# Thirty-three loads issued by ScalarE instead of SyncE, in a gated linear attention kernel with a low-rank mixer and an MLP behind it

## The chip, the cores and the metric

The kernel runs on one core of a Trainium2 chip. The metric is device time in microseconds (us) of one execution, the median of several runs. The engines that compute are TensorE (PE), VectorE (DVE), ScalarE (ACT) and GpSimd (POOL); SyncE (SP) computes nothing and issues transfers. Each engine works through its own stream of instructions in order; semaphores tie the streams together. An instruction that starts a transfer (a DMA) stands in the stream of the engine that issues it, and the transfer itself is carried out by 16 DMA engines.

## What is computed

The batch is 4, with 8 heads, 768 steps and a head size of 48, so that the model's width is 384. A recurrence with a gate per channel is followed by a mixing over time with a matrix of rank 32 and an MLP of width 1536:

```python
for t in range(S):
    state = alpha[:, :, t, :, None] * state + np.einsum('bhd,bhe->bhde', k[:, :, t], v[:, :, t])
    y[:, :, t] = np.einsum('bhd,bhde->bhe', q[:, :, t], state)
x = y.transpose(0, 2, 1, 3).reshape(B, S, H * D)
h = x.transpose(0, 2, 1) @ U @ V
u = x + h.transpose(0, 2, 1)
out = u + np.maximum(u @ w_ch1, 0.0) @ w_ch2
```

Inputs and output are float32; the matmuls run in bfloat16.

## The kernel before

**Tiles.** The sequence of each batch is cut into six chunks of 128 steps. Every chunk needs four tiles of 128 x 384 float32 (192 KB each): alpha, k, q and v. The four batches have 96 such tiles. 24 more tiles of the same size bring the MLP's weights (12 for `w1`, 12 for `w2`), and U and V come in four small transfers. All tiles of this size, and the output's, live in a pool `io` of 40 slots; a load that takes a used slot waits until the last reader of the tile that lay there is done.

**A chunk's work.** Two forms of the recurrence exist. `stage_pair` handles the first chunks of batches 0 and 1 (six and four chunks: the list `PAIRS`); its tiles are loaded with rows of two steps (L332, "paired" in what follows). `stage_gla` handles the others (L339, "unpaired"). In both, ScalarE takes the logarithm of alpha (Ln, L362 or L534), TensorE sums it up over the chunk, ScalarE takes Exp of the sum with both signs (L385 and L386, or L551 and L552), and VectorE or GpSimd multiplies k and q by these (L393 or L562). The products `rkq` are transposed to `kqt`: by TensorE and an eviction (L411, L576, then a copy), except for batch 3, whose six transposes are done by the DMA engines (L588). Then come the scores (L435, L604), their masking on VectorE (L446, L614), the update of the state (L469, L627, and what follows), and the output y (L508, L518, L666, L671), which is evicted to `xb`.

**Behind the recurrence.** `stage_mix` mixes over time with U and V (L686, L716, and for batch 0 L705 and L708) and brings `uT`, the transpose that the MLP reads; for batch 3 this transpose is done by the DMA engines (L722). `mlp1` has 24 groups of three matmuls of 128 x 384 for each batch (L767), each evicted with Relu by ScalarE (L777) or VectorE (L779). `mlp2` has for each chunk twelve matmuls in three groups (L793), a sum on VectorE (L799) and the store of the output (L802, L804): two stores of 96 KB for a paired chunk, one of 192 KB for an unpaired one, and the very last chunk is split in two column ranges.

**What sets the order.** The functions do not emit instructions: each adds steps to a list (`Plan.add`, with the engines that could do the step). A step is a function with its engine to be chosen; it may emit one instruction or a group of matmuls. A text `TABLE`, written in advance, then lists all 1071 steps, three characters each: two name the step and one its engine. A second text `SLOTS` gives the slot of each buffer at its first use. `Plan.run` walks through the table and emits. Thus the table sets the order of every engine's stream; between engines only the semaphores count, so that an engine may be far ahead of another one's place in the table. SyncE, which waits for nothing but free slots and finished results, can be far ahead with its loads. In the kernel before, all 123 loads, the nine transposes and the 35 stores are in SyncE's stream, 167 entries.

Lines to follow: `weight` (issue on L305, its conversion to bfloat16 by L273 on ScalarE or L277 on GpSimd), `stage_loads` (L332 and L339), `copy` (L273 on ScalarE, L275 on VectorE, L277 on GpSimd).

Of the kernel before, what the change touches and what calls it, by code (L numbers as in the profile page):

```python
# [15 lines left out]
TABLE = """
A8SCcABASCzABQSETACePChACfAA+SCgACjDC1PC4AC3AC2AEVPEYABISA9SCiDCkPCmDClPBBSC5GEXADjADlPDnAEWACnDDmACoPCqDA-SCdGCrPCsDBDS
C0GDCPBCSC6GC7PBESCvPCpDC8PC+DDKACtPCuDCwPCxDDDDC9AC-PDADDBDABSAFGAGPAHDAJPAKADMPDPABKSCyDDEPDNADGPDFDDqGDsPBJSDpGDrPDtA
DuDDHPDJADZPBYSG2ABSSEaGBHSDLGDoAEcPDyPEeADIDBFSDQGDaPDbDDSPDUDDvPDwDBMSBLSDkGDzPD0DDxDG4PD8AD+PBRSEZGEbPEdDD3PDcPDdDDOA
BGSDRGDTPDVDG5AEAAD1PD2DBUSGfABOSEDGEfPEhDEgDD-AG7ABNSECGEBAG6ABTSBcSEUABPSD9GGhPGiAGjAGkAD4PELPBVSBWSGlGGmGBgSBXSGgGAAS  # L20
ADGBZSG8GAiSAjGAQSAeSAfGAgSAhGDWPDXDEiPD5PD7ABkSD6AEjPEkDEFPEEPEHAHNADYDEGDElPEMPENDAOSAPGARGEmPDfPAMSANGDePEnPEoADgPDiD
DhAAYSAZGBaSG9GAWSAUSAVGEIPEJDEKDHmAHPPHSAEPPGnPAXGASSATGHQABdSHTGBbSG3GEpAHRABiSBfSHOGAaSBhSBeSBoSAcSAkSBlSBjSAmSBpSAoS
BqSBmSGoPGqDGpDEOPAqSBnSHoPHrAEQPESDAuSAsSGuPGvDGwDEqPGrPGtDGsDERAErPHpAHqAHtGE8PE5PAwSAySEwPG+PHADE2PBrSEsAExPEyAE6PE7D
FFPE9PE+DA2SE3PEtPEzPFBPFCDFHPEuPFJPFGDE4AEvAE0PE1AF1PH-AFIDGyPF5PF3PF4DE-PFADFfPFgDF6AF2AFDPFhPFiAGxDFlPFmAFdPA4SACSFED
A0SFKDFLPFMAFNPFODG-PFjPFkAFeDA6SFVPFWAIBPICAFRPFSAHUGHBDHCPHDDAdGBsSGzPIEAIDAHFPFtPHGDHHDHIGIGGG0AAbAFuAHVPHXAG1AFnPHJP
B0SBwSBySB4SB8SFPPBuSBzSFQAHEDHKPHLAHMAHcPHdDHeDHsDIFAIVAFTPFUAFoAFrPFsAFpPHvPFqDHfDHxAHWPIXPIYAHuPHwDFvPFwDFZPFaDFzPF0D
HYAHiPHZPHbDHaDIZAAnAHyPHzDIHDFbPApAFcAHhPFxPFyAFXPHjPHkAHlAFYAHnGH1PH2DH3DH4DIIPIKAH6PAlGIaGIcPIbGIdPIfAIJPArGGTPIeAH7P
GNPH0DH8PH+AILDIMPH9DIODIgPIhDGBPIAGIPPH5GIRDF7PGZPHgGAzGAtAAvAAxAGOPINDITPF8PIQDIiDISGIWAIjPA5GGaPA3AGCPIUAAEGIkAIlPImD
GUPA1GA7AGbPGcDIvPIwDALGIzPI0DI1PI2DF9PF+DItPIuDGDPKLAGPPInPIpPIqDGEDKNPK0AI3PIxPIyDIoDKfAKOAI4AKPAKhPKjAKnGGVPGWDK2PK3A
LJAKlAJfPJgALeAKRAIrPIsDJRPJjPJSAJkDJdPJeAKiAKkAK6AKQAI5PJHPJIDJPPJQAJLPJMAI-PJAAK5AK4ALgPLkAJFPJGDJJPJKDLjABxSKmGKoPKqA  # L30
JTPJUDI6DKTGKVPJnPJoDLiALhABvSKMGBtSKSGKgAKUPJXPKWDKXDKbPKcDJlPLLPLMAJYDJbPJmAB9SB2SK8GKvPJBPK+PKwDKxDLAACASJcDJDPJEAB1S
KpPKrDGQDLOAK7GLNAJCAI9PI+ALPACESK9PK-DCMSNlAI7PI8DJVPJWALzAB3SK1GKsPKuDLBPLDDLCDKYPKZDJvPJNPJOAB6SLRGLTPLVAJhPL1PL2AL3A
B+SCCSB5SLHPLIANnPNqAB-SKtDLfALlGLnPKaDJwPL5GLQDCBSL4GLEPNrAKyPKzAJiAOIAB7SLKALpAGHPJZPGIPLSPLUAJaALFDLGGLmGKBPL6PL8DGJP
L7PGKDL9ALoPLqACNSCISCFSNoANsGLZPLaDJxPJyDNpACGSNtGKCPCKSCLSCQSCUSCDSLWPLXDL+PLrPKdPKeALYDLtDKDPJ7PLuPN2AN4PN5AJ8PJpPLbG
LsDLvDL-DLwGMADL0GOaAOcPOgAOfAOdACHSNmGN3GLcPN6ALdAN+GJ9PLxPLyDKEDMBPJqPNuSNvPNwDMCAMDPJrPOeAGMSNxDJ+DMEAN7AN8AOKPOMAAIG
MTPMUDMNPJ1PMLPMRPKGPMODJsDMMDCSSCRSOhGNyPNzDN0PMHPMIDKHPMFPMGDOsAOuPKIPMPPMQAMSDMJPMKDOOAMVPMWDKJDJ2PCWSOvAOLAMfPMXPMYD
J3PMjPM7POiGCYSO+AGFSCTSGGSPAPN1AONAObGGYSCJSCXSOtGCaSGSSKFSGLSN9GOwACPSOjSCVSOzGO0DOPDMkDMgDOxAOyAPBAPCAMbPMcDMpPMqAMlP
MmAJ4DNBPODPNDPMZPM-POEDMaAM8ANCACOSOQGNADM1PM2AOkPM5PNEDMxPMyAN-SM9PMhPM3PM4AJuSF-SMtPM6AMuAOJGOVPCZSPDGPEDOmDOlDOFDOWD
OXGMdPMeDM+AOnPOoDOpGNFPNGDMnPMoAMvPMiAOqPOrAOAPOBDO1SO2PO3DO4DOCDORSJ-SOSPOUDNHPMrPMsANRPMzPO5PO6DO7GOTDO8PO9ANSPGRSCbS
O-APFSJ5SPGPM0DPIDPHDGXSOGPOHANTPNUDOYPMwANIPPJPPKAOZAGASNJPNbPPLPNMPNcPPMAPPPPQDPSPPXPPNPPODPRSPYDPTDNdPNKDPUPPVDPWSNWP  # L40
NgPJtSNNPPZPNhPPaDPbSNXPNiPNOPNeDJ6SNPDNQSJzSNVSKASGeSGdSNYPNfSNLSNjDNkSPmPPePPuPPvAPgPPiPPjDPcPP2PPyPPnAQCPNZDNaSPoPPwP
PhAPzAPxAP3DQAPQBAPdAP8PPkPPlDP6PQGPQHAQIPQJDQEPQKPQFAQDAPsPP4PP5AP0PPtDP+PPfAPqPP1DPpAP-AQWPQMPQRPPrDQLDQNPP7AP9AQlPQXP
QSPQqPQYPQZDJ0SKKSQaSQrPQbPQTPQUDQVSQmPQOPQPDQQSQsPQtDQuSQcPQnPQoDQpSQgPQdPQhPQeDQfSQiPQjDQkS
"""
SLOTS = """
AABBCCAAADAABBBBCCEFDAEGBCAFACAGHAHAABAIBDEJCKHABBGABCABBGDDLBCCGMACBHNCODPCAEADQAGCCABFCRSDEDHACTBABUDAAVBWBFBABBXDCYZE
aAGCBACDbcCdeBfAghijEHBBkBFGBCCDlEAmBnABCFHCAGCDCDBFDEDAGHEIJKLMNOPQRSTUBCAVWFDYXHEBAGBCACBBADabHEDFZAAGcCBEAHDFBAECAGBH
EFCdeGBEFfHDAGBCBgFACEHGABCBBAEFijlkhHmnGCBADCAHGCABFDBAEHGBCACBEFADHGACCDBCBECGAHBDCAEDBFBHCCEAGBFHBBBGCBABBGCCHABGBCBF
HBCCAGBDDEAABFBCDHBAHBCFBAHGCCABAFHAGBEBBBEDHEAHBGACFCBIGAAEGACCKHLCJDAAMGOBBHCPCCDAGEBAFCBHQCDDEGACNSRHCABTABDDUCGAVBCF
HGBDCEADWGXYbBAHAaAZcdefgEFBDHGBAAEACFCBBBCACBGCAiEDACDDjHBADBHBkADCAGCAHFDElhFCGCABFCGBCFADmEBAFBADEHBGBABnLAPCQDMBABCB  # L50
ACGIDBFCAAKHGBCECADFHCESDADBBBGAAFCEHABCAGCBBFDAHAGCABBBTEDDABBRFCABEBDAGCFAUBDFCOVNGHBBCAEFBGbADCFBDCEBCEBGEBHGAEBZDYeg
iFd
"""


# [91 lines left out]
def kernel(  # L147
# [37 lines left out]
    nc.scalar.preload_act_table_set("natural_log_exp_and_others")

# [115 lines left out]

    def weight(dst, src, key, engs):
        t = Buf(io)
        P.add({"SP": 545.0}, lambda e: nc.sync.dma_start(flat(t), src), w=[t])  # L305
# [20 lines left out]
    def stage_loads(b):  # L326
        def load(t, src, c):
            if paired(b, c):
                hs, sl = slice((c % 2) * HP, (c % 2 + 1) * HP), slice((c // 2) * 2 * C, (c // 2 + 1) * 2 * C)
                P.add(  # L330
                    {"SP": 775.0},
                    lambda e: nc.sync.dma_start(  # L332
                        t().rearrange("p (h j) d -> p h (j d)", j=2), src[b, hs, sl, :].rearrange("h (p j) d -> p h (j d)", j=2)
                    ),
                    w=[t],
                )
# [2 lines left out]
            P.add({"SP": 1100.0}, lambda e: nc.sync.dma_start(t(), src[b, :, sl, :].rearrange("h t d -> t h d")), w=[t])  # L339
# [518 lines left out]
```

## Time and profile before

| | |
|---|---|
| runs shown | 159.73, 161.85, 162.47 us; median 161.85 |
| span of the profiled execution | 161.6 us |
| instructions in the profile | 4518, of them 1728 matmuls |
| HBM read and written | 23.89 MB and 4.72 MB, 177 GB/s over the span |
| chain of waits, share of the span by engine | PE 54%, SyncE's queue 20%, DMA 14% |

In the profile's lines, PE, DVE, ACT, POOL and SP are the engines, PEld is the loading of weights into TensorE, a "q" behind an engine's name is its issuing side, L332 is line 332, `out<-in` names the tile that is written and the tile or tensor that is read, and "xN" counts instructions. Times are us unless marked ns. A busy share of the DMA engines can come out a little over 1, since their packets overlap. A busy TensorE is not a TensorE at its peak, as the ends of overlapping matmuls are modelled.

### The profile page before, as it was taken

The numbers are of one execution on the slowest core, as the hardware profiler recorded it, in microseconds if no ns is written. First come the engines' busy times: TensorE is split into PE (matmuls) and PEld (weight loads), VectorE is DVE, ScalarE is ACT, GpSimd is POOL, SyncE is SP. The second block draws the span as 40 slices with busy tenths as digits, with TensorE's granted clock in tenths as the row PEclk, the third lists the DMA queues.
The fourth block names the chain that finished last, engine by engine and source line by source line (L and its number), as shares of the span: only waits on it lengthen the run. The fifth ranks groups of instructions, "written<-read, shape, count | busy, mean of one in ns | idle before, by whom it ended". The sixth has DMA issues, their size and how long they took to land.

```text
span 161.6 us, 4518 instructions
## 1 busy us (share of the span) xinstructions
PE 149.2 (92%) x1728; PEld 98.7 (61%) x1728; DVE 105.7 (65%) x232; ACT 90.8 (56%) x234; POOL 66.0 (41%) x104
## 2 busy tenths in 40 slices
...
DMA  4999995999999969889999899999992047840034
GB/s 125 289 312 315 248 250 150 268 336 253 285 229 279 293 130 209 176 176 203 207 195 215 160 189 198 195 226 204 146 204 67 0 81 172 262 146 0 0 129 163
DMA packets 96964, 31.05 MB, mean 192 GB/s; under 512 B 90640, under 2 KB 96912, under 8 KB 96944
## 3 DMA queue, kind: packets, MB, share of 16 engines
q1 hardware_dynamic: 96944, 30.78, 81.2%
...
HBM read 23.89 MB, written 4.72 MB: 177 GB/s over the span
## 4 chain that ended last, share of the span: by engine, by line
PE 54%; SPq 20%; DMA 14%; issue 4%; POOL 3%; DVE 2%; ACT 1%; POOLq 0%; DVEq 0%
PE ps L793 24%; PE ps L767 19%; SPq L332 13%; DMA io<-in_q_dram 5%; SPq L339 3%; DMA kqt<-rkq 3%; DMA io<-in_moe_w_ch_dram 2%; DMA io<-in_k_dram 2%; DMA io<-in_v_dram 2%; PE ps L576 2%; SPq L802 2%; SPq L305 2%; PE ps L604 1%; PE ps L716 1%; DVE pm L614 1%
## 5 line engine op out<-in xcount | busy, mean ns | idle before, releaser
L767 PE MATMUL ps<-uT,w_sb 128*128 128x384 bf16 x288 | 53.2, 326 | 0.4 <-POOL w_sb L277 0.4
L793 PE MATMUL ps<-w_sb,h1t 128*128 128x384 bf16 (+2 forms) x300 | 53.1, 319 | 0.0
L777 ACT ACTIVATE h1t<-ps 128x384 bf16<-128x384 f32 x61 | 27.6, 497 | 23.2 <-PE ps L767 23.1
L793 PEld LDWEIGHTS <-h1t 128*128 128x128 bf16 x300 | 27.1, 97 | 15.6 <-issue 0.8
L767 PEld LDWEIGHTS <-w_sb 128*128 128x128 bf16 x288 | 26.5, 98 | 16.4 <-POOL w_sb L277 1.2
L779 DVE TENSOR_SCALAR h1t<-ps 128x384 bf16<-128x384 f32 x35 | 18.6, 553 | 14.2 <-PE ps L767 14.2
L799 DVE TENSOR_TENSOR io<-ub,ps 128x384 f32<-128x384 bf16 (+2 forms) x25 | 13.3, 533 | 10.2 <-PE ps L793 10.0
L614 DVE TENSOR_TENSOR pm<-ps,maskc 128x512 bf16<-128x512 f32 x28 | 17.7, 682 | 1.1 <-PE ps L604 1.1
L562 POOL TENSOR_TENSOR rkq<-io,ai 128x384 bf16<-128x384 f32 x12 | 11.4, 949 | 13.8 <-DMA io<-in_k_dram 8.5
L717 DVE TENSOR_TENSOR ub<-xb,ps 128x384 bf16<-128x384 bf16 x24 | 12.4, 548 | 4.5 <-PE ps L716 4.3
L446 DVE TENSOR_TENSOR pm<-ps,maskp 128x512 bf16<-128x512 f32 x20 | 13.1, 683 | 2.4 <-PE ps L435 2.4
L562 POOL TENSOR_TENSOR rkq<-io,aa 128x384 bf16<-128x384 f32 x11 | 10.0, 912 | 9.8 <-ACT aa L552 8.4
L273 ACT CAST xb<-ps 128x192 bf16<-128x192 f32 (+1 forms) x27 | 10.3, 404 | 6.3 <-PE ps L671 4.9
L277 POOL CAST rv<-io 128x384 bf16<-128x384 f32 x18 | 9.4, 529 | 10.3 <-DMA io<-in_v_dram 9.3
L277 POOL CAST w_sb<-io 128x384 bf16<-128x384 f32 x16 | 8.0, 518 | 7.5 <-DMA io<-in_moe_w_ch_dram 7.5
L273 ACT COPY kqt<-ps 128x512 bf16<-128x512 bf16 x17 | 9.8, 610 | 1.9 <-PE ps L576 1.2
L275 DVE COPY kqt<-ps 128x512 bf16<-128x512 bf16 x19 | 7.8, 420 | 4.0 <-PE ps L576 2.2
L551 ACT ACTIVATE ai<-ps 128x384 bf16<-128x384 f32 x14 | 6.9, 498 | 5.5 <-PE ps L543 3.6
L411 PE MATMUL ps<-ident,rkq 128*128 128x128 bf16 x80 | 8.2, 237 | 1.6 <-DVE rkq L393 1.0
L393 POOL TENSOR_TENSOR rkq<-io,ai 128x384 bf16<-128x384 f32 x8 | 7.3, 910 | 5.8 <-DMA io<-in_k_dram 5.8
L638 POOL TENSOR_TENSOR st<-sm,tot 128x384 bf16<-128x384 f32 x7 | 5.8, 829 | 6.6 <-DVE sm L654 6.6
L393 POOL TENSOR_TENSOR rkq<-io,aa 128x384 bf16<-128x384 f32 x9 | 8.2, 910 | 0.6 <-DMA io<-in_q_dram 0.3
...
## 6 DMA issues: line engine op xcount, KB each, us to landing
...
```

Source lines behind the costliest of these rows:

```text
L273: nc.scalar.copy(dst, src)
L277: nc.gpsimd.tensor_copy(dst, src)
L332: lambda e: nc.sync.dma_start(t().rearrange("p (h j) d -> p h (j d)", j=2), src[b, hs, sl, :].rearrange("h (p j) d -> p h (j d)", j=2)),
L393: eng.tensor_tensor(jh(dst()[:, :, 0:D]), raw(a), jh(x()), op=ALU.mult)
L446: nc.vector.tensor_tensor(dst, s2, maskp.to_broadcast([C, 2, 2, C]), op=ALU.mult)
L562: eng.tensor_tensor(dst()[:, :, 0:D], a(), x(), op=ALU.mult)
L614: nc.vector.tensor_tensor(pm()[:, :, par, :], s2, maskc.to_broadcast([C, HP, C]), op=ALU.mult)
L767: nc.tensor.matmul(hb()[:, 0:TW], lhsT=w1_sb[:, ct, jt * 128 : (jt + 1) * 128], rhs=u_half(uT, ct, tt, b in QUEUE_U), start=(ct == 0), sto ...
L777: nc.scalar.activation(dst, hb()[:, 0:TW], AF.Relu)
L779: nc.vector.tensor_scalar_max(dst, hb()[:, 0:TW], 0.0)
L793: nc.tensor.matmul(hb()[:, 0 : hi - lo], lhsT=h1()[:, jt, c * C : (c + 1) * C], rhs=w2_sb[:, jt, lo:hi], start=(jt == 0), stop=(jt == NJ - 1),
L799: P.add({"DVE": 468}, lambda e, hb=hb, lo=lo, hi=hi: nc.vector.tensor_tensor(flat(ou)[:, lo:hi], ub()[:, c, lo:hi], hb()[:, 0 : hi - lo], ...
```

## The change

A new helper gives the queue that belongs to a step's engine, and the three load steps may now name ScalarE. The list `SUM_U` takes the place of a test for batch 0 and holds just batch 0, so that nothing changes by it. Everything else is in the two texts, which are replaced as a whole. No step is added or removed, and no tile changes its shape or its way of being loaded.

```diff
+    SUM_U = (0,)
...
+    def queue(eng):
+        return nc.scalar if eng == "ACT" else nc.sync
...
     def weight(dst, src, key, engs):
         t = Buf(io)
-        P.add({"SP": 545.0}, lambda e: nc.sync.dma_start(flat(t), src), w=[t])
+        P.add({"SP": 545.0, "ACT": 450.0}, lambda e: queue(e).dma_start(flat(t), src), w=[t])
...
                 P.add(
-                    {"SP": 775.0},
-                    lambda e: nc.sync.dma_start(
+                    {"SP": 775.0, "ACT": 450.0},
+                    lambda e: queue(e).dma_start(
...
-            P.add({"SP": 1100.0}, lambda e: nc.sync.dma_start(t(), src[b, :, sl, :].rearrange("h t d -> t h d")), w=[t])
+            P.add({"SP": 1100.0, "ACT": 450.0}, lambda e: queue(e).dma_start(t(), src[b, :, sl, :].rearrange("h t d -> t h d")), w=[t])
...
-        if b == 0:
+        if b in SUM_U:
```

Read step by step, the new table differs from the old one in this:

- **Queues.** 33 of the 123 loads are issued by ScalarE: nine tiles of batch 0 (alpha of chunks 0 and 2; q of chunks 0, 2, 3 and 5; v of chunks 3, 4 and 5), two of batch 1 (k and v of chunk 2), ten of batch 2, nine of batch 3, and three tiles of `w2`. Thirteen of them stand in the table ahead of the first MLP group on TensorE. ScalarE's first two entries that concern data are the loads of alpha and q of chunk 0, and the load of chunk 2's alpha follows; they stand behind the table load of its functions (L185), which is emitted first of all.
- **Engines.** Of the steps that compute, ScalarE has 217 (233 before), VectorE 228 (209), GpSimd 86 (89), TensorE 373 as before. Of the 96 evictions of `mlp1`, ScalarE has 54 (61 before) and VectorE 42 (35).
- **Order.** The first MLP group of batch 0 is entry 274 of the table (297 before) and needs 37 of the transfers in the order in which they are listed (38 before). Batch 3's last tile stands on SyncE behind five stores and four DMA transposes (eleven stores, one of them of 192 KB, and five transposes before). Behind the first use of that tile stand 249 matmuls of full width (128 x 384, the split last chunk counted as such) on TensorE, behind that of the old order's last tile 214.
- **Slots.** The slots of all buffers are chosen anew. For each load on ScalarE that takes a used slot, the step that frees it stands at least 73 entries ahead.

More of the change, by code (lines that the diff above doesn't have):

```diff
@@ L16 @@
 TABLE = """
[L17 to L40, printed above, removed]
@@ L41 @@
-NgPJtSNNPPZPNhPPaDPbSNXPNiPNOPNeDJ6SNPDNQSJzSNVSKASGeSGdSNYPNfSNLSNjDNkSPmPPePPuPPvAPgPPiPPjDPcPP2PPyPPnAQCPNZDNaSPoPPwP
-PhAPzAPxAP3DQAPQBAPdAP8PPkPPlDP6PQGPQHAQIPQJDQEPQKPQFAQDAPsPP4PP5AP0PPtDP+PPfAPqPP1DPpAP-AQWPQMPQRPPrDQLDQNPP7AP9AQlPQXP
-QSPQqPQYPQZDJ0SKKSQaSQrPQbPQTPQUDQVSQmPQOPQPDQQSQsPQtDQuSQcPQnPQoDQpSQgPQdPQhPQeDQfSQiPQjDQkS
+BASA8ABISBCSBBSA9SA+ABEACzAC1PC2ACcACePBDSBJSBQSDjADlPC3AC6GC8PCfACiGBKADoAC5DC7PA-SC+DC9DC-PBGABFSBRSBMSCgACjGClPCkPBHS
+BLADnABUSBSADADDBDDKADMPDmABNSC0ADCPBYSCmDCnDDpGC4ADDDCoPDEPCpDCqDDrPDtDBOSBPADPAETAEVPChADOABTABgSDqGDGPDsPDNABWSDuDABS
@@ new lines @@
+BVSBcSAASDHPEWABXSCdGCrPEXADJACsDDFDDvPDwDEYAD8AAQSCtPCvPCwPCyDCxABkSAOSAMSBaSDRGDTPDIACuDDVAAgSDQGAiSD+PD-ADyPAeSEZGDSP
+EBADxDDUDEbPEdDDLGDZPDaPDbDDWPDXDEAADkGDzPD0DDcPDdDBZSGfAGhPGiAGjAEaGEcPEeDD3PDYDD1PBhSD4PD5PEfPEhDASSAYSBiSAUSD2DEgDG2A
+GkAD7AD6AECGEEPEGADfPG4PG6AG7AAWSAcSEDGEFPG5AELPDePHmAElPEiPD9GEMPEHDENDDgPEUGEjPEkDEIPBbSDiABwSEJDEKDBeSEmPEPPHoPEOPAaS
+BjSBdABoSDhDGmGGoPHqAEnPHNAEQPERDGlGGnPESAGpDHPPAFGAJPGqDAGPAHDHpAADGEqPEpAGrPEoAErPGtDHrAGgAGuPGvDGwDEzPGsDAKAE5PEtPEsA
+E6PE0PE1DE8PARGGyPE2PE9PEuPE3PE4DBfABlSE7AFDPBpSEvDEwPBsAE+AGzPG0ABqSBmSAkAAhAExPEyAFEDG1AANGFHPFIDAPGFjPGxDFnPFlPFmDFoD
@@ new lines @@
+FJPFKDFkAHRAFLPH-AAmSAjGAfGFfPFBPFCDAqSAoSAsSFdPG8GG+PFeAHQAAwABnSFgAFMDHADHtDHsGAySAuSF5PBrSFhPF3PF4DF1PHuPHwDFiAA0SACS
+AVAG9GG-PF2AHSAHBAHvPHxDF6DFNPFOAA2SA4SIBPIEAIDAICAKfAHyPHzDATGHCPHEDE-PFADHDDA6AB0SH0DAXGAZAAdGFtPFRPFTPFuAIFAFVPFWAFSA
+CASHUGHWPHYDAbGFzPF0DKhPKjAKiAG3GHFPHGDHHDHnGH1PIVAHIDH2DH3DH4DFpPFqAHTGFxPFyDHVPKkAHXAKlAFvPFUDFwAIXPIZAIYAFrPHJPFsDFXP
+FYAHKPHMAHOGHcPHdDHLDHeDHZPHaDKLAIGGHbDH5GIIPIKAFbPFcAKNPKRAKOAIaGFZPKQAH7PHfDIcPIbGIdPIfDHhPFPPFaDKPAHiPIeAH6PFQAIHGIJP
+ILDArAHjPHlDHkAH8PH9AIgPIhDH+DIMPIODINDAlGAnGFFPFGDBuAApGGTPGNPAtGF7PGBPGZPB8AIAGIPPAxAAzAAvGGUPIWAHgDITPIUAIRDIQDISGGCP
@@ new lines @@
+GaPIiDIjPALGGOPAEGIkAIlPF8PBvSBxSImAItPI1PI2DIvPIwDA7GA5GA3GA1AF9PIpPIqDIuDBzAKgGGPPGQDCESGDPGEDLzAK0AK2PIzPInPIoDBtALeA
+K6AK5AK4AI0DGVPGWDIxPIyAIrPIsDI3PGbPKTGB2SB1ABySCQAB3SJNPLgPLhAI5PI6AI4DGcDF+DLjANlAJHPKmDKSDJTPJnPJoDK3AK7GCCAKoPKqDKMG
+B4SJOAJLPL1PLiAL2AJUDJdPJMDJeDJPPJQDJJPJbPCBSJcDLkAB9AJKAB+SJZPK8DCMAJjPJkACFSI7PI8AL3AJaAOaAJBPJCDB5SCXSCGSKbPKcDK9PK-D
+JhPJDPJXPKvPKwDJiAKnGKpPJIAI-PJADJYDJEALJAB6AKrDK+PLAAKVPJRPJSAKUPKWAJFPJGALLPLPALMAKXDB7SLBPLCDLDDKsPKYPCDALOAKtDLlGKxG
+LNAB-SGHPJlPKZDNnPNqALmGNrALnPGIPLpAJmAKaDI9PNoAI+ANpACUSJVPJWAKuDLoPLqDL5DL4GK1GLEPL6PJ1PCHSKdPKeALFDOcPNsDLrPLtDLsDKyP
@@ new lines @@
+GJPGKDCOACVAKzALQGLKGLRGLZPLSPLUACaSLHPLIDL7PJ2PL9DLGGLaDNtGAIGNuSCISLfAL8ALTPLVAJfPJgDJ3PLuPLbGLvDLwGOsAJ4DOuPOwAOxACNA
+OIACPSCJSLWPLYDLXDOyAL+PMADCKSNmGKBPL0GOdALxPLyAJvPKCPOeACYAOvAN2ALcPLdACLSL-DNyPNzDMBPCWSKDPMCDOfAOKPOgAKEDOLAOPGNvPNxD
+OMAMDPN4PMEAN5ACZANwDOQGORSJ7POJAMHPMIDMNPMTPN6AN3AONAMRPMSDMODJwPN0PMLPJ8PMFPMUDMVPJ9PMMDMPPMGDN1DOtGMJPN+GN9DCbSN-SOzG
+JxPMQDJ+DMWAM-PM3PM4AMKDO0DM1PJyDO1SOOANAAO+AMxPMyDMrPM2DN8AN7AODPNBPOEDMpPGYSCSAOiGMnPMoAMqDCRANCAMjPMkDJpPMZPMaAMsDOSP
+OAPOBDOUDOTDOCDOFDO2PO4DJqPPAPPCAPBAGGSGdSGFSNDPNEAJrPJsDMdPMhPOYPM9PM7PM8AMtPMXPMYAO3DM+AMiAOZDMuDOVPOWDM5POXDM6DMbPMlP
@@ new lines @@
+MmAMvPMfPMcDMgDMzPGSSCTSObAOhGOnPMeAOoDOGPPDGOjSOkPOlDM0AMwAPEGPFSPGPPHDO5POpGO6DNFPKGPO8PO9AKHPNGAOmDOqPOrAO-GNWPO7GPID
+PJPKFSGRSGeSNXPPKAOHDPLPNRPPMAPSPPTDPUPPVDPWSPZPPaDNgPPXPPYDJ-SNMPNbPKIPKJDPbSPPPPQDNNPNSPPNPPODNhPNOPNcPNYPNTPNUDNdPNeD
+QEPNZDQCPQGPQHDNPDNHPQIPQJAJuSPRSPgPPcPPePPfDQFDPdDQDDP8PNiPNjDPsPP+PP-DPmPPiPP4PKASPhDQAPQBANVSKKSGASP9APqPPjDQWPPwPJtS
+GMSGXSNkSPkPNIPPlAP5DF-SP0PP1AJzSPoPPpANJPPnAPrAGLSNfSJ6SPuPPvDP6PQMPP2PP3APxDNKDP7AQNPQXPNLSJ0SPyPNaSQlPQRPPzDNQSQqPQSP
+PtDQYPQTPQUDQKPQrPQZDQaSQOPQPDQVSQLAQsPQtDJ5SQQSQuSQmPQbPQnPQoDQcPQgPQdPQeDQpSQfSQhPQiPQjDQkS
@@ L44 @@
 """
 SLOTS = """
[L46 to L49, printed above, removed]
```

12 lines of the change are left out of this document (8 added, 4 removed).

## The prediction

> **What bounds the kernel now.** I read the page first (spans, busy shares, the DMA digits), then the chain of waits in order of time, then the busy times by stretch, and last the rows of the issuing lines on the DMA queue.
>
> ```profile
> span 161.6 us, 4518 instructions
> ...
> PE 149.2 (92%) x1728; PEld 98.7 (61%) x1728; DVE 105.7 (65%) x232; ACT 90.8 (56%) x234; POOL 66.0 (41%) x104
> ...
> DMA  4999995999999969889999899999992047840034
> ...
> q1 hardware_dynamic: 96944, 30.78, 81.2%
> ```
>
> TensorE is busy for 92% of the span and no other engine comes near. The DMA digits are the second thing to see: nearly all nines for three quarters of the span, then a fall. All of it runs on one queue, q1, which SyncE issues. So there are two candidates for the bound, and the chain tells where each one rules. Its columns are start, length and what the chain ran through.
>
> ```profile
> 1.23 0.49 SPq L332
> ...
> 24.70 1.88 SPq L305
> ...
> 27.58 3.94 DMA io<-in_moe_w_ch_dram
> ...
> 114.06 4.30 DMA kqt<-rkq
> 118.41 0.40 PE ps L604 x8
> ...
> 126.53 0.43 PE ps L686 x6
> ...
> 135.20 11.70 PE ps L767 x72
> ...
> 158.73 0.30 DVE io L799
> ```
>
> Up to 31.5 (27.58 + 3.94) the chain is SyncE issuing loads and the first MLP weight landing: the fill. From then on it is mostly TensorE. Shortly before 118.41 it leaves TensorE again, for batch 3's loads and transposes. After 118.41 it is TensorE to the end, at full density: 72 matmuls in 11.70 us are 0.1625 us each. The last eviction starts at 158.73, so 2.9 us at the end are eviction and store.
>
> ```profile
> core 0: us, PE busy (x) PEld busy (x) DVE busy (x) ACT busy (x) POOL busy (x), PEclk, DMA share, GB/s
> 0.00:31.60 31.60, 24.22 (x461) 18.41 (x461) 23.46 (x72) 21.21 (x58) 19.80 (x39) 1.00 0.92 242
> 31.60:105.00 73.40, 72.66 (x850) 48.09 (x849) 53.93 (x108) 52.28 (x137) 38.43 (x57) 1.00 0.98 220
> 105.00:118.40 13.40, 12.11 (x107) 7.15 (x105) 9.40 (x19) 6.80 (x17) 6.98 (x8) 1.00 1.10 199
> 118.40:158.70 40.30, 40.21 (x314) 25.09 (x314) 18.63 (x36) 10.46 (x24) 0.83 (x1) 1.00 0.39 105
> ...
> 70.00:90.00 20.00, 20.00 (x242) 13.97 (x241) 15.89 (x31) 15.88 (x42) 11.49 (x14) 1.00 1.04 205
> ```
>
> The busy times by stretch give the room. TensorE's idle time is 7.4 us in the fill, 0.7 in the 73 us after it, 1.3 in batch 3's wait and 0.1 behind it. The granted clock is 1.00 throughout. Since overlapping matmuls count as busy, the true loss is larger where the matmuls are small. The DMA engines stand at a share of 0.92 in the fill and at 0.98 and 1.10 up to 118.4: there is next to no transfer capacity to be won, only an order to be improved.
>
> **The change part by part.** Thirty tile loads and three weight loads leave SyncE's stream and enter ScalarE's; their bytes, patterns and slots' number stay. Read out of the new table, 13 of the 33 stand ahead of the first MLP group on TensorE (nine of batch 0, two of batch 1, one of batch 2, one weight), the other 20 later.
>
> ```profile
> L332 SPq DMA_DIRECT2D io<-in_q_dram x10: 378/506/2044, 2.3 to 37.8; - x10
> ...
> L339 SPq DMA_DIRECT2D io<-in_alpha_dram x14: 383/865/2937, 28.1 to 96.1; - x14
> L339 SPq DMA_DIRECT2D io<-in_k_dram x14: 378/661/2807, 40.8 to 111.6; - x14
> ```
>
> These rows give least, median and longest time of one issue on SyncE: 0.51 us for a paired tile and 0.66 for an unpaired one (its lower median; the other holds waits); a weight, with as few rows as a paired tile, I count at 0.51 too. The longest, 2.0 to 2.9 us, are issues that were held up. No row shows an issue on ScalarE. I take SyncE's medians, because the instruction is the same; the lower end is zero (it may run while an earlier ACTIVATE still computes), the upper end a held-up issue.
>
> *The fill.* 12 x 0.51 + 0.66 = 6.8 us of issuing enter ScalarE's stream ahead of the first MLP group. ScalarE is busy for 21.2 of 31.6 us there, so 10.4 us are free to cover it, but not freely: an issue that stands in front of an Exp delays that Exp, the product on VectorE or GpSimd behind it and the transpose on TensorE behind that. What leaves SyncE costs nothing there, and the first weight could be issued earlier. But the bytes ahead of it are about the same (37 transfers are needed in the new order for the first MLP group, 38 in the old), and the DMA engines already stand at 0.92, so at most 8% of 31.6 us, 2.5 us, can come out of a fuller queue.
>
> ```profile
> 0.73 1.28 ACT L185 ACT_TABLE_LOAD   x1 [0.73 <-PEq L842]
> 3.42 1.11 ACT L362 ACTIVATE lt<-io 128x384 bf16<-128x384 f32 x2 [1.40 <-DMA io<-in_alpha_dram]
> ```
>
> The very start gains nothing: ScalarE's first issue stands behind its table load, at 2.0 us, where SyncE issued its second tile at 1.23; the first Ln waits for a tile that SyncE still issues first. Bounds of the fill: -2.5 to +6.8 us. I take 0, as the cover of 10.4 us is larger than the 6.8 and the transfer engines are nearly full.
>
> *From 31.6 to 105 us.* The 20 later issues are 18 x 0.66 + 2 x 0.51 = 12.9 us. ScalarE has 73.4 - 52.3 = 21.1 us free; its busy share would go from 71% to 89%. Sixteen computing steps also leave it and 19 come to VectorE, which has 19.5 us free here. None of ScalarE's loads waits long for its slot: the step that frees it stands 73 or more steps ahead in the table. Bounds 0 to +12.9 us. TensorE lost 0.7 us here with ScalarE at 71%; I take it that this doubles, +0.7, since the nearest row is that of the hidden case.
>
> *Batch 3's wait.* In the old order 11 stores and five transposes stand ahead of the last load on SyncE; in the new one five stores and four transposes do.
>
> ```profile
> 117.05 0.59 SPq L339 DMA_DIRECT2D io<-in_v_dram  x1
> ...
> DMA to landing us min/median/max: 2.8/3.7/6.0
> ...
> L767 PE MATMUL ps<-uT,w_sb 128*128 128x384 bf16 x58 | 10.4, 326 | 0.0
> ```
>
> The six stores (five of 96 KB, one of 192 KB) are 0.69 MB and the transpose 0.26 MB, which at the 205 GB/s of the row for 70 to 90 us is 3.4 + 1.3 = 4.7 us of DMA time that no longer precedes the last tile. That tile was issued at 117.05 and landed about 3.7 later, near 120.8; batch 3's mixing starts at 126.53, so it had up to 5.8 us to spare. In the new order 249 matmuls of full width stand behind the first use of the last tile, against 214 behind the old one: it is wanted 35 x 0.1625 = 5.7 us earlier. 5.8 + 4.7 - 5.7 leaves 4.8 us in hand, so no new wait on the last tile is due. What can be won is what TensorE loses from 105 to 118.4: at least the idle 1.3 us; at most 13.4 - 58 x 0.1625 = 4.0, if the 49 small matmuls there cost nothing. At 0.05 each (eight took 0.40 in the chain) they take 2.4, and the loss is 1.6. I take all of that: -1.6. Bounds -4.0 to 0.
>
> *The end.* The last 2.9 us stay: the same split store of the last chunk. 0. The new split of evictions (ScalarE 54 of the MLP's 96 instead of 61) changes nothing where both engines wait for TensorE.
>
> **Rule and trace.** The row: one queue moves 30.78 MB and holds the engines at 0.98 to 1.10 until 118.4 us. The Trainium skill, "DMA: Bandwidth & Descriptors", section "Issuing engines are not separate DMA queues", says that transfers started by scalar, sync or gpsimd run on the same 16 engines and interleave, and that a second issuer saves only the time of initiating. By that rule the sum has no term for a higher transfer rate, as mine has none; it is the third rival below where it is carried to its end.
>
> **Sum.** 161.6 + 0 + 0.7 - 1.6 = 160.7 us of span. The median of the runs shown, 161.85, stands 0.25 above the profiled span; 160.95, so 161.0.
>
> **The rivals.**
>
> *Faster: the queue was the limit in the fill.* For it: the held-up issues (1.88 us at 24.70 in the chain, in front of the first weights), while the DMA share of the fill is under 1. With two queues the gap closes: -2.5, the middle at 0, batch 3 -1.6, which gives 157.5 + 0.25 = 157.7. Against it: ScalarE, which has to feed the fill's Exp, pays for it.
>
> *Slower: ScalarE becomes the engine that paces the fill.* Its 21.2 us of work and 10.4 of waiting are a chain (tile, Ln, prefix sum, Exp), and the 6.8 us of issuing are put into this chain rather than into its gaps. Then the first MLP group comes up to 6.8 us later and nothing takes it back, since TensorE is dense behind it: 160.7 + 6.8 - 0.7 + 0.25, about 167.0. It decides from +4.9 us on (165.1 - 160.2), or ten of the thirteen issues fully in the way; below that the result stays within 2%. Against it: the moved issues are spread out between ScalarE's steps, three at the front, and ten microseconds are free.
>
> *No effect.* The DMA engines set the pace up to 118 us in both kernels, the issue time that SyncE saves was hidden behind them, and ScalarE's gaps hide what it takes on: about 161.9. For it speaks the DMA share of 0.98 over 73 us; against it that fewer stores stand ahead of the last tiles.
>
> **How the numbers follow.** The forecast of 161.0 gets 0.33, no effect 0.12, faster at 157.7 gets 0.25, slower at 167.0 gets 0.30. Two per cent, about what a measurement of this kernel can tell from no change, are 3.2 us: under 158.6 is faster, over 165.1 slower. So 0.25, 0.45 and 0.30. The range takes in the faster case with a part of the larger end for batch 3 (down to 156.5) and the slower one (up to 167.5); outside lie the held-up issues on ScalarE and the full 4.0 us. The likeliest case alone spans 159.5 to 162.5.
>
> **What would show it.** The page should list a second DMA queue, with ScalarE issuing at 0.45 to 0.7 us each; issues of 1.5 us or more there speak for the slower rival. The first matmul of the MLP (L767, some lines lower then) should start at 31 to 32 us: 29 says the faster rival, 34 or more the slower one. TensorE's idle time in the 13 us before batch 3's mixing should be under 0.5 us, and the last tile should land near 116 us. Idle in the middle should stay under 1.5 us; if ScalarE is named as what ended TensorE's waits there, the +0.7 was too small. The forecast is wrong if the last matmul does not end 2.9 us before the span's end, or if the mean DMA share from 5 to 110 us is under 0.9.

## The result, and the profile after

The changed kernel takes 167.33 us (median of four runs, 166.54 to 167.73) against 161.37 us of the kernel before in the same comparison (four runs, 159.73 to 162.47). The ratio is 1.039, with a 95% interval from 1.033 to 1.045: slower. The forecast was 161.0. The page of the profiled execution (167.73 us, span 165.8) has these lines in the place of those shown before:

```profile
span 165.8 us, 4488 instructions
...
PE 151.4 (91%) x1728; PEld 100.9 (61%) x1728; DVE 115.3 (70%) x251; ACT 84.0 (51%) x218; POOL 63.7 (38%) x101
...
PEclk9999999999999999959999999999999999999999
DMA  5999989999989999899924899996700546334062
...
q1 hardware_dynamic: 70944, 24.29, 64.5%
q10 hardware_dynamic: 26000, 6.49, 18.4%
```

The second queue is there (q10, 6.49 of 30.78 MB), ScalarE does less (84.0 us, 90.8 before), and yet the span is 4.2 us longer. The averages don't say where. The busy times by stretch do; the columns are as in the prediction:

```profile
core 0: us, PE busy (x) PEld busy (x) DVE busy (x) ACT busy (x) POOL busy (x), PEclk, DMA share, GB/s
0.00:31.60 31.60, 24.80 (x472) 19.09 (x473) 23.21 (x70) 20.09 (x56) 20.24 (x40) 1.00 1.02 278
31.60:105.00 73.40, 69.84 (x805) 46.47 (x804) 58.44 (x118) 48.35 (x126) 37.43 (x55) 0.98 1.05 204
105.00:118.40 13.40, 13.08 (x116) 8.00 (x114) 11.50 (x22) 5.89 (x16) 3.93 (x4) 1.00 0.91 181
...
65.00:70.00 5.00, 3.14 (x27) 1.98 (x26) 3.56 (x8) 0.95 (x4) 0.00 (x0) 1.00 0.81 152
70.00:75.00 5.00, 4.32 (x17) 1.98 (x17) 1.67 (x3) 2.73 (x8) 2.20 (x3) 0.66 1.33 235
```

TensorE is busier than before in the fill (24.80 against 24.22 us) and in batch 3's wait (13.08 against 12.11), and loses in between: 69.84 against 72.66 us, at a granted clock of 0.98 instead of 1.00. Most of that lies in the ten microseconds from 65 to 75: TensorE idle for 1.9 and 0.7 us, ScalarE busy for only 0.95 us in the first five and GpSimd for nothing at all, and after the hole a clock of 0.66 over five microseconds, which is up to 1.7 us of work not done. In the kernel before, the first of these stretches was full:

```profile
65.00:70.00 5.00, 5.00 (x41) 3.19 (x40) 2.24 (x5) 4.87 (x16) 1.98 (x3) 1.00 0.78 155
```

The timeline of ScalarE in the changed kernel shows what happened there (start, length, line, operation; in brackets the idle time ahead and what the profile takes for its end):

```profile
58.95 0.48 ACT L274 CAST utx<-ps 128x384 bf16<-128x384 f32 x1 [0.64 <-PE ps L690]
58.96 0.37 ACTq L343 DMA_DIRECT2D io<-in_v_dram  x1
...
63.91 0.80 ACT L274 COPY uT<-ps 128x768 bf16<-128x768 bf16 x1 [0.53 <-PE ps L740]
67.94 0.43 ACTq L343 DMA_DIRECT2D io<-in_k_dram  x1
68.41 0.59 ACTq L343 DMA_DIRECT2D io<-in_alpha_dram  x1
69.05 0.49 ACT L555 ACTIVATE ai<-ps 128x384 bf16<-128x384 f32 x1 [4.34 <-PE ps L580]
```

ScalarE ends its work at 64.71, computes nothing for 4.34 us and goes on only after two issues. The bracket names TensorE (L580), but what stands between is the issue at 67.94. The issue itself lasts 0.43 us. What it waited for is not in the row, and it is in the program: the landings of the loads, stores and transposes are counted on eight semaphores, which the built program hands out in turn over both queues, and a transfer on a semaphore waits until the earlier transfer on the same one has landed, whichever engine issued it. For ScalarE's 18th to 24th load, read from the built program:

```
load by ScalarE       waits for the landing of (eight ahead in the built order)
18  batch 2 c1 v      batch 2 c4 alpha   (ScalarE's 17th)
19  batch 2 c0 k      batch 3 c0 alpha   (SyncE)
20  batch 2 c2 k      batch 2 c3 alpha   (SyncE)
21  batch 3 c3 alpha  batch 2 c1 v       (ScalarE's 18th)
22  batch 2 c5 q      batch 3 c0 k       (SyncE)
23  batch 2 c4 k      batch 2 c2 k       (ScalarE's 20th)
24  batch 3 c2 alpha  batch 3 c3 alpha   (ScalarE's 21st)
```

Laid beside the trace, 16 of ScalarE's 30 issues that have a transfer eight ahead start 0.02 to 0.04 us after its landing, among them the 18th, 19th, 20th, 22nd and 23rd. In the kernel before none of SyncE's 160 did: the shortest distance there is 0.16 us, so this wait decided nothing. Of the seven in the list only the 20th and the 22nd keep ScalarE from computing for more than 0.3 us, by 3.2 and 0.6 us. The 21st follows right behind the 20th, and the 24th starts 0.36 us after its landing.

The transfer for which the 20th waits is SyncE's issue at 62.24, and its row gives the time from the start of the issue to the landing:

```profile
L343 SPq DMA_DIRECT2D io<-in_alpha_dram x1: 1217/1217/1217, 62.2 to 62.2; - x1
...
DMA to landing us min/median/max: 5.7/5.7/5.7
```

62.24 + 5.68 = 67.92 (the last two digits from the trace), and ScalarE's issue starts at 67.94. The chain of waits runs through the next one of this kind, the 22nd load:

```profile
64.96 0.28 SPq L343
65.34 1.65 SPq L343
67.08 4.34 DMA io<-in_k_dram
71.45 0.40 ACTq L343
71.89 0.50 ACT h1t L781
```

SyncE issues batch 3's chunk 0 k at 67.08, it lands 4.34 us later at 71.42, ScalarE's issue starts at 71.45, and behind it in ScalarE's stream stands an eviction of the MLP (L781), for which TensorE waits. This became theory H (held): ScalarE's issues wait for landings and hold every Exp and eviction behind them. Its rivals were theory I (the issues cost by the time that they take), theory O (the new order costs, not the queue) and theory F (the fill, the slower rival of the prediction).

### The profile page after: what moved, and what is told of

Read it like the earlier page. It is cut to its first block, busy times and chain, and to the rows that moved or that the text cites. A ratio compares the mean times of both kernels' runs of the same rounds, so it can differ in the third digit from the quotient of the medians.

```text
span 165.8 us, 4488 instructions
## 1 busy us (share of the span) xinstructions
PE 151.4 (91%) x1728; PEld 100.9 (61%) x1728; DVE 115.3 (70%) x251; ACT 84.0 (51%) x218; POOL 63.7 (38%) x101
## 3 DMA queue, kind: packets, MB, share of 16 engines
q10 hardware_dynamic: 26000, 6.49, 18.4%
## 4 chain that ended last, share of the span: by engine, by line
PE 62%; DMA 19%; SPq 7%; DVE 4%; ACT 3%; issue 2%; POOL 1%; ACTq 0%; POOLq 0%
PE ps L797 25%; PE ps L771 24%; DMA io<-in_k_dram 7%; DMA io<-in_alpha_dram 6%; DMA io<-in_moe_w_ch_dram 3%; SPq L336 3%; DMA io<-in_v_dram 3%; PE ps L720 2%; PE ps L580 2%; PE ps L608 2%; PE ps L675 2%; DVE pm L618 1%; SPq L343 1%; SPq L309 1%; PE ps L670 1%
## 5 line engine op out<-in xcount | busy, mean ns | idle before, releaser
L771 PE MATMUL ps<-uT,w_sb 128*128 128x384 bf16 x288 | 55.2, 332 | 2.4 <-ACT h1t L781 2.2
L797 PE MATMUL ps<-w_sb,h1t 128*128 128x384 bf16 (+2 forms) x300 | 54.0, 320 | 0.0
L781 ACT ACTIVATE h1t<-ps 128x384 bf16<-128x384 f32 x54 | 25.5, 495 | 38.1 <-PE ps L771 36.7
L771 PEld LDWEIGHTS <-w_sb 128*128 128x128 bf16 x288 | 27.5, 99 | 20.9 <-issue 5.5
L783 DVE TENSOR_SCALAR h1t<-ps 128x384 bf16<-128x384 f32 x42 | 22.0, 553 | 16.4 <-PE ps L771 16.4
L566 POOL TENSOR_TENSOR rkq<-io,ai 128x384 bf16<-128x384 f32 x10 | 9.3, 926 | 21.0 <-ACT aa L556 7.8
L274 ACT CAST xb<-ps 128x192 bf16<-128x192 f32 (+1 forms) x23 | 8.5, 391 | 6.4 <-PE ps L675 6.3
L276 DVE COPY kqt<-ps 128x512 bf16<-128x512 bf16 x24 | 9.7, 418 | 1.5 <-ACT ai L389 0.5
L278 POOL CAST rv<-io 128x384 bf16<-128x384 f32 x17 | 8.7, 523 | 4.7 <-DMA io<-in_v_dram 4.7
L375 PE MATMUL ps<-lt,upto 128*128 128x384 bf16 x10 | 4.1, 406 | 5.8 <-ACT lt L366 5.8
L397 POOL TENSOR_TENSOR rkq<-io,ai 128x384 bf16<-128x384 f32 x9 | 8.4, 937 | 2.6 <-ACT ai L389 2.1
L555 ACT ACTIVATE ai<-ps 128x384 bf16<-128x384 f32 x14 | 7.0, 498 | 4.7 <-PE ps L580 4.3
```

What stands on the lines that cost most here:

```text
L276: nc.vector.tensor_copy(dst, src)
L397: eng.tensor_tensor(jh(dst()[:, :, 0:D]), raw(a), jh(x()), op=ALU.mult)
L566: eng.tensor_tensor(dst()[:, :, 0:D], a(), x(), op=ALU.mult)
L771: nc.tensor.matmul(hb()[:, 0:TW], lhsT=w1_sb[:, ct, jt * 128 : (jt + 1) * 128], rhs=u_half(uT, ct, tt, b in QUEUE_U), start=(ct == 0), sto ...
L781: nc.scalar.activation(dst, hb()[:, 0:TW], AF.Relu)
L783: nc.vector.tensor_scalar_max(dst, hb()[:, 0:TW], 0.0)
```

## The experiments

Two of the experiments rearrange entries of the table (the rearranged list and the eight later loads), and three add copies to it; in the others its order is kept, and an edit is shown as the entries whose engine changes. Kernels of one group ran on the same chip beside the kernel before; from group to group the kernel before differed (median 161.7, 162.1, 163.5, 164.4 us), so ratios are compared and not times.

### All loads back on SyncE

```diff
-  all 33 loads        ACT
+  all 33 loads        SP
```

> The new table with all 33 loads given back to SyncE, at their places in the list; order, engines of the other steps and slots stay. Theory H (held by landings): in the changed kernel an issue on ScalarE starts only when the transfer eight places earlier in the list has landed, whichever queue carried it (the issue at 67.94 us starts 0.02 us after a tile that SyncE issued at 62.24 landed), and ScalarE's Exp and evictions wait behind it. Then the ratio to the kernel before is 0.99 to 1.015. Theory I (issue time): the 33 issues of 0.4 us on ScalarE are the price; same ratio here. Theory O (order): SyncE's new order, whose first transpose of batch 3 waits 9.8 us (79.8 to 89.7) with the rest of the loads behind it, and the new engines make it slow: 1.03 to 1.04. Theory F (my slower rival, the fill): 0.99 to 1.01.

1.012 [1.005, 1.019], and in a second measurement of five rounds:

> All 33 loads on SyncE in the new order, once more with five rounds beside the kernel with the copies: the base for the price of issue time. All theories: 1.005 to 1.019. If the new order costs anything by itself, the interval stays over 1.

1.010 [1.006, 1.014]. Theory O explains somewhat over a quarter of the loss, if the new order has to be issued by SyncE alone; the rest comes with the queue.

### The thirteen early loads, or the twenty later ones

```diff
 late_sp:
-  20 later loads      ACT
+  20 later loads      SP
 early_sp:
-  13 early loads      ACT
+  13 early loads      SP
```

> The new table with the 13 early loads left on ScalarE and the 20 later ones given back to SyncE. H: the fill has room for its holds (TensorE's first MLP matmul comes at 31.8 us in both kernels), so 0.99 to 1.015, like all_sp. I: a third of the price stays, 1.01 to 1.02. O: 1.03 to 1.04. F: all of it stays, 1.03 to 1.04.

> The reverse: the 13 early loads on SyncE, the 20 later ones on ScalarE. H: the loss of 65 to 75 us stays, 1.025 to 1.04. I: two thirds of the price, 1.02 to 1.03. O: 1.03 to 1.04. F: 0.99 to 1.01.

With the 13 early loads alone on ScalarE 1.012 [1.005, 1.019], the same as with none: theory F falls, the fill pays nothing for them. With the 20 later loads alone on ScalarE 1.030 [1.020, 1.041], inside H's band and at the edge of I's and O's. The cost hangs on these loads; by what mechanism, this run alone does not tell.

### Two of them back

```diff
-  batch 2 c2 k, batch 3 c3 alpha      ACT
+  batch 2 c2 k, batch 3 c3 alpha      SP
```

> The new table with just two loads given back to SyncE, those that ScalarE issued at 67.94 and 68.41 us (k of batch 2's chunk 2, alpha of batch 3's chunk 3). H: ScalarE's idle 4.3 us ahead of them and the hole of TensorE behind go, unless the next load on ScalarE is held in their place: 1.005 to 1.02 if it goes, 1.03 if the hold moves on. I: 31 of 33 issues stay, 1.035 to 1.04. O: 1.035 to 1.04. F: 1.035 to 1.04.

1.026 [1.017, 1.035], between H's two cases and below the 1.035 of the others. The busy times by stretch of this kernel:

```profile
65.00:70.00 5.00, 4.71 (x35) 2.79 (x34) 4.15 (x10) 2.03 (x6) 1.57 (x3) 1.00 0.95 165
70.00:75.00 5.00, 3.96 (x29) 2.48 (x29) 2.66 (x6) 1.90 (x5) 0.65 (x1) 1.00 1.11 218
75.00:80.00 5.00, 3.13 (x32) 2.21 (x31) 2.15 (x6) 3.66 (x10) 1.57 (x2) 1.00 1.35 218
```

The hole from 65 to 70 shrinks from 1.9 to 0.3 us and comes back at the next of ScalarE's issues: 1.0 and 1.9 us in the next ten. One hold hides the next.

### The queue alone, on the old order

The old table, engines and slots; only the same 33 loads go to ScalarE, at their old places.

> The old order, engines and slots of the kernel before; only the same 33 loads are moved from SyncE's stream to ScalarE's, at their old places in the order. Theory H (an issue on ScalarE waits until the transfer eight ahead in the list has landed, and holds ScalarE's stream): 1.015 to 1.04 of the kernel before, ScalarE named as what ended holes of TensorE in the stretch after 31 us, issues on ScalarE starting within 0.05 us of the landing eight ahead. Theory O (the new order is what costs): 0.99 to 1.005. Theory I (the issue's own time on ScalarE, 33 x about 0.4 us): 1.01 to 1.03, with issues that start as soon as the step ahead of them ends. Theory F (the fill): first MLP matmul 2 us or more later than before.

1.309 [1.296, 1.322], far beyond every theory's bounds:

```profile
span 207.4 us, 4492 instructions
...
PEclk9998555665899789999969999999889999999999
...
PE 50%; DMA 22%; issue 11%; POOL 7%; ACT 4%; DVE 2%; SPq 1%; ACTq 0%; POOLq 0%; DVEq 0%
```

The old table lists loads at places at which SyncE does not stand, as it runs ahead as far as slots allow. On ScalarE a load has to wait until the steps ahead of it have been passed, and is then late for its reader (DMA 22% of the chain, 14% before). Only three of ScalarE's 33 issues start within 0.05 us of the landing eight ahead, where H had expected that of the issues in general, and the granted clock is low as well (0.90 over the span). So this run shows late loads more than held ones and does not separate H from O. It shows that a table made for SyncE's running ahead can't be given to ScalarE, and that the new order, against theory O, is what makes the second queue bearable at all.

### The issue's time without its wait

All loads on SyncE, and 20 copies on ScalarE at the later loads' places:

```diff
+    scratch = const.tile([C, 2, C], BF16, name="scratch")
+    P.dummy = lambda: nc.scalar.copy(scratch, maskc.to_broadcast([C, 2, C]))
```

> All 33 loads on SyncE in the new order (the kernel that measured 1.012); at the 20 later places where ScalarE issued a load it makes a copy of 128 x 256 elements into a tile that nothing reads, about 0.4 us each, about as long as an issue there. It has the issue's time on ScalarE and none of its waits. Theory I: as much as the 20 later issues cost, 1.025 to 1.04. Theory H: 1.010 to 1.018, no more than the kernel without the copies. Theory O: 1.012. Theory F: 1.012.

> The same with 20 copies of 128 x 256 elements on ScalarE at the places of the 20 later loads, once more with five rounds. Theory I: its ratio stands 0.015 to 0.025 over that of the kernel without the copies. Theory H: 0 to 0.008 over it. The first measurement, 1.022 against 1.012 in different runs, is compatible with both.

1.022 [1.013, 1.030] at first, which left H and I both possible; with five rounds 1.016 [1.012, 1.020] beside 1.010 for the kernel without copies on the same chip. The difference of 0.006 lies in H's band; from the two intervals it is known to about 0.006 either way, which still stays below the 0.015 that theory I asked for. The price of 20 such pieces of time on ScalarE is then about 1 us, a sixth of the loss.

### A list that changed nothing

> The changed kernel with every engine's stream as it is: the same instructions in the same order on each engine, the same 33 loads on ScalarE. Only the list from which the program is built is rearranged: SyncE's loads from about 30 us on stand up to 80 entries later in it, which puts older transfers eight ahead of ScalarE's issues (mostly ScalarE's own earlier ones), and moves the waits to SyncE. Theory H: 1.00 to 1.025, fewer and shorter holes of TensorE ended by ScalarE from 65 to 75 us, where the changed kernel lost 4.3 us. Theories I, O and F: 1.03 to 1.045, as the changed kernel, since nothing that they count is altered.

1.034 [1.023, 1.045]. This does not speak against H, because the edit did not do what it was made for: the built program gives the semaphores in an order of its own, not in the table's, and here it came out with the same 4498 instructions (of the whole built program) and the same predecessors as the changed kernel. It is a second measurement of the changed kernel, useful for one thing:

```profile
65.00:70.00 5.00, 3.40 (x27) 2.11 (x26) 3.35 (x8) 1.41 (x5) 0.33 (x1) 1.00 0.96 175
70.00:75.00 5.00, 4.32 (x26) 2.43 (x25) 3.02 (x5) 2.76 (x9) 2.23 (x3) 1.00 1.36 231
```

The holes are there again (1.6 and 0.7 us), but no drop of the clock; the span is 163.7. The dip to 0.66 is not part of every execution.

### Eight loads later in ScalarE's stream

```diff
 ScalarE's stream:
-  20th load, 21st load, L555, L781, L558, L538, L555, 22nd load
+  L555, L781, L558, L538, L555, 20th load, ...
   (and the 21st to the 27th load likewise, six computing steps later)
```

> The changed kernel with eight of ScalarE's loads (the 20th to the 27th that it issues, those from 67 to 88 us) moved five or six computing steps later in ScalarE's own stream, behind the steps that they held up; nothing else is moved, every load stays on ScalarE. Theory H (the issue waits for a landing and holds the steps behind it): 1.005 to 1.028, the hole of TensorE from 65 to 72 us gone or under half, since the steps run while the landing is still out. Theory I (issue time) and theory O (order): 1.03 to 1.045 as the changed kernel, as the same issues take the same time in the same stretch.

1.028 [1.023, 1.033]: just inside H's band, with an interval that reaches into the others', and the hole did not vanish. The timeline of ScalarE and the busy times by stretch of this kernel:

```profile
68.38 0.49 ACT L555 ACTIVATE ai<-ps 128x384 bf16<-128x384 f32 x1
71.31 0.37 ACTq L343 DMA_DIRECT2D io<-in_k_dram  x1
71.73 0.49 ACT L781 ACTIVATE h1t<-ps 128x384 bf16<-128x384 f32 x1 [2.86 <-DMA io<-in_q_dram]
```

```profile
65.00:70.00 5.00, 5.00 (x45) 3.30 (x43) 4.27 (x10) 2.61 (x6) 1.38 (x2) 1.00 0.79 134
70.00:75.00 5.00, 2.61 (x16) 1.36 (x14) 2.77 (x6) 1.89 (x5) 0.00 (x0) 1.00 1.07 213
```

TensorE is now full where the hole was, and idle for 2.4 us five microseconds later, at the moved issue, which got a later transfer as its predecessor: it starts at 71.31, and the landing that it waited for was at 71.29. The hold moves with the issue.

### Seven of them back

```diff
-  ScalarE's 18th to 24th load      ACT
+  the same seven                   SP
```

> Seven of the 20 later loads (the 18th to the 24th that ScalarE issues, from 59 to 75 us, where all issues started at a landing) go back to SyncE; 13 later ones and the 13 early ones stay on ScalarE. Theory H: 1.010 to 1.022, next to the kernel with all loads on SyncE, no hole of TensorE over 0.5 us ended by ScalarE from 60 to 80 us. Theory I: seven twentieths of the cost go, 1.026 to 1.034. Theory O: 1.03 to 1.045.

1.001 [0.997, 1.006], below H's band and far below the others'; once more, on another chip:

> The kernel with seven of the 20 later loads back on SyncE, once more, as the base for the two kernels with added waits: 0.997 to 1.008.

0.999 [0.994, 1.004]. H had expected the 1.2% of the kernel with all loads on SyncE to stay. The loss hangs on seven instructions of 33, taken together. The busy times of the first of the two:

```profile
65.00:70.00 5.00, 5.00 (x39) 3.17 (x38) 4.27 (x10) 3.33 (x9) 1.97 (x3) 1.00 1.05 205
70.00:75.00 5.00, 5.00 (x44) 3.32 (x42) 3.33 (x8) 3.77 (x10) 1.17 (x2) 1.00 1.05 201
```

and TensorE's groups from 62 to 76 us, of the changed kernel and then of this one (line, form, count, busy time and mean, idle time ahead):

```profile
L771 PE MATMUL ps<-uT,w_sb 128*128 128x384 bf16 x37 | 8.2, 373 | 2.2 <-ACT h1t L781 2.2
...
L580 PE MATMUL ps<-ident,rkq 128*128 128x128 bf16 x4 | 0.4, 220 | 0.0
```

```profile
L771 PE MATMUL ps<-uT,w_sb 128*128 128x384 bf16 x56 | 10.2, 326 | 0.0
...
L580 PE MATMUL ps<-ident,rkq 128*128 128x128 bf16 x20 | 1.8, 219 | 0.0
L631 PE MATMUL ps<-rv,rkq 128*128 128x96 bf16 x8 | 0.7, 206 | 0.0
```

In the same 14 us the changed kernel does 19 matmuls of L771, 16 of L580 and 8 of L631 less. At 0.1625 us for 384 columns, and in proportion for 128 and 96, that is 3.1 + 0.9 + 0.3 = 4.3 us, of a difference of the spans of 165.8 - 160.7 = 5.1 us.

### The wait without the issue

Moving loads moves waits and issues together. The last two kernels start from the one with seven loads on SyncE and add to ScalarE, at the old place of the 20th load (and in the second kernel also of the 22nd), a copy that reads a tile still on its way:

```diff
+    scratch = const.tile([C, 5, D], BF16, name="scratch")
+    P.touch = lambda t: nc.scalar.copy(scratch, t[:, 0:5, :])
```

> As the kernel with seven loads back on SyncE, no issue added to ScalarE; at the place where the changed kernel's ScalarE issued its 20th load it makes one copy of 128 x 240 elements out of the tile of batch 2, chunk 2, v, which in the base landed at 68.1 us, some 3.5 us after ScalarE is there. A wait for a landing without an issue. Theory H: a hole of TensorE of 1.5 to 4 us near 65 to 70 us, ended by ScalarE; 1.008 to 1.025, at least 0.008 over the base. Theory I (issue time, one copy of 0.4 us): no more than 0.003 over the base.

> The same with a second such copy, at the place of the 22nd load, out of the tile of batch 2, chunk 3, alpha, which in the base landed at 70.1 us. Theory H: as the kernel with one such copy or up to 0.012 over it, since the second landing comes 2 us after the first; theory I: no more than 0.005 over the base.

One copy: 1.013 [1.001, 1.026], where the base beside it has 0.999; two: 1.017 [1.006, 1.028]. The intervals are wide. That of two copies lies above the base's, that of one copy overlaps it, so the trace has to carry the verdict. ScalarE's timeline and the busy times by stretch with one copy:

```profile
64.80 0.80 ACT L284 COPY uT<-ps 128x768 bf16<-128x768 bf16 x1 [0.53 <-PE ps L750]
68.87 0.39 ACT L277 CAST scratch<-io 128x240 bf16<-128x240 f32 x1 [3.28 <-DMA io<-in_v_dram]
69.17 0.48 ACT L565 ACTIVATE ai<-ps 128x384 bf16<-128x384 f32 x1
```

```profile
65.00:70.00 5.00, 4.00 (x36) 2.58 (x34) 4.27 (x10) 1.72 (x5) 0.00 (x0) 1.00 0.97 191
70.00:75.00 5.00, 4.62 (x28) 2.70 (x28) 3.05 (x6) 3.45 (x11) 3.10 (x4) 1.00 1.00 196
```

A wait of 3.28 us and 0.39 us of work put the hole back at its place: TensorE idle for 1.0 and 0.4 us where the base had 0.0, GpSimd without work from 65 to 70, as in the changed kernel. No load is issued by ScalarE between 54 and 76 us here. That a wait for a landing on ScalarE, without an issue, makes this hole is shown. Its price, 0.014 over the base, is a good third of the loss and known only roughly. That the waits of the seven loads make up all of it is inferred from the kernel without them, which moves their transfers as well, and is not shown by itself.

## Why the prediction was wrong

**The step that failed** is the term for the stretch from 31.6 to 105 us: "+0.7, since the nearest row is that of the hidden case", with "the held-up issues on ScalarE" left outside the range. They are what happened. Counting every matmul at its dense time (0.1625 us for 384 columns, smaller ones by their distances in full stretches) and taking the sum from the time that passed, TensorE lost 5.2 to 5.9 us more in this stretch than before, where the forecast allowed 0.7. This is an estimate; its width comes from the times set for the small matmuls. The half clock behind the hole is in it: in the second execution of the same program, which had no such dip, the same count gives about 4 us. TensorE's idle time there is 73.40 - 69.84 = 3.6 us, over the 1.5 that the prediction had set as a sign, and 2.2 us of it end at ScalarE's eviction L781.

Its argument was that a load on ScalarE waits for its slot, and that the slots are free early. That was right and not enough: a load also waits for the landing of the transfer eight ahead. With SyncE as the only issuer that landing had always come: eight issues at SyncE's medians take 4.1 to 5.3 us and a landing 3.7 to 3.9, so that one issuer hardly meets the wait (an estimate from the rows of the kernel before). With two issuers SyncE meets it too, in the fill above all, but nothing that computes stands behind its loads. On ScalarE, Exp and evictions of the MLP do.

The price was also looked for in the wrong column. The forecast bounded the hold by the longest issues on SyncE (2.0 to 2.9 us) and wrote that issues of 1.5 us or more on ScalarE would speak for the slower rival. The issue that cost the most lasted 0.43 us. The Trainium skill, "Perfetto Trace Analysis", section "DMA Instruction — HWDGE (DVE, Sync)", says that the profiled window of such an instruction opens only when all its semaphores are satisfied, and this trace agrees: the 4.34 us of idle time lie ahead of L555, not within the row of the issue. The trace of before did not name a landing as what released SyncE's loads, as none did, so the wait could not be read off there; that the loads are issued with a bounded number on the way could have been asked.

The other steps, with the same count of TensorE's loss:

| step | forecast, us | measured, us | |
|---|---|---|---|
| fill, to 31.6 (35 in the count) | 0 (-2.5 to +6.8) | -0.6 to +0.2 | right; first L771 at 31.62, first L767 before at 31.44 |
| 31.6 (35) to 105 | +0.7 (0 to +12.9) | +5.2 to +5.9 | failed, within its own bounds |
| batch 3's wait, 105 to 118.4 (120) | -1.6 (-4.0 to 0) | -1.8 to -2.2 | right |
| behind it, to the last eviction | 0 | -0.1 to +0.3 | right |
| end | 0 | +0.8 | last eviction at 162.07, 3.7 us before the end; the last store is issued 0.4 us after the eviction's end, at once before, and lands 2.2 us later instead of 1.7; why is not known |
| sum | -0.9 | about +4.2 | spans: +4.2 |

**The very start.** The first issue on ScalarE was put behind the table load, at 2.0 us. It ran beside it:

```profile
0.73 1.28 ACT L186 ACT_TABLE_LOAD   x1 [0.73 <-PEq L846]
0.77 0.47 ACTq L336 DMA_DIRECT2D io<-in_alpha_dram  x1
```

That issues may run while an earlier instruction computes was named as the lower end, and it held here and at 58.96 above.

**Batch 3.** The idle time from 105 to 118.4 is 13.40 - 13.08 = 0.3 us, as "under 0.5" said, and the last tile, issued at 110.79, landed at 114.1 (116 forecast). This agrees with the argument of the fewer stores ahead of it; no run takes the stores apart from the rest of the new order.

**The rivals.** The slower one gave 167.0, and 167.33 was measured, but its mechanism, ScalarE pacing the fill, was wrong: the 13 early loads cost nothing (1.012 with and without). The number agreed by chance. The faster rival's gap in the fill did close (DMA share 1.02, 278 GB/s, against 0.92 and 242), but it was worth 0.6 us at most and not 2.5: the kernel with all loads on SyncE moved 244 GB/s in the fill and started its first L771 at 31.19, earlier than the changed kernel. Over the middle stretch two queues moved 204 GB/s, one queue 220. That the rate was higher in the fill and not in the middle fits the rule weighed in the prediction, by which only the time of initiating is saved; no run tests the capacity of two queues by itself.

**The base.** The spans differ by 4.2 us, the medians by 6.0. Around the span of the changed kernel lie 1.9 us, so the profiled execution of the kernel before, with its span of 161.6, took some 163.5: one of its longer ones. The kernel before, run once more, bears this out. It was expected at 0.99 to 1.01 and came to 1.003 [0.997, 1.010]; its profiled execution took 163.72 us with a span of 161.9, 1.8 us less. The 1.8 us between the two differences can't be found by laying the two traces beside each other. The 0.25 in the prediction's sum sets a median against the span of another, longer execution, and is not what lies around a span. As a difference from the median, the forecast of 161.0 stands at -0.9 all the same, so this is not where it failed.

**What stays open.** The new order costs about 1% when SyncE issues all of it, and nothing when 26 loads stay on ScalarE. Whether those 26 gain 1%, or the order suits a divided stream only, no run separates. No kernel tried beats the one before by more than its interval.
